# A second guessed expert, and 512-row units, in a fused attention and mixture-of-experts kernel

## The chip, the cores and the metric

The kernel runs on one core of a Trainium2 chip. The metric is device time in microseconds from launch to end; lower is better. Before and after are compared as medians of runs on the same chip. The engines are named as the profile names them: PE (TensorE, matmuls), ACT (ScalarE), DVE (VectorE), POOL (GpSimd, which issues the indirect transfers) and SP (SyncE, which issues the plain ones).

## What is computed

Three stages follow each other on 2304 tokens of 512 values. The cut reference:

```python
x = attn(q, k, v)                    # 4 x 8 heads, 576 positions, causal window of 64
h = maximum(x @ w_in, 0)             # 512 -> 2048
x = h * h @ w_out                    # 2048 -> 512, dense, all tokens
logits = x @ w_gate + modality_bias[modality_id]       # 8 experts
e_idx = argmax(logits); gate = max(softmax(logits))
for e in range(8):                   # top-1 mixture of experts
    m = e_idx == e
    out[m] = gate[m] * (maximum(x[m] @ w1[e], 0) @ w2[e])   # 512 -> 1024 -> 512
```

All arithmetic is fp32. The kernel gets it from matmuls on a high and a low part of each operand: three passes (high x high, high x low, low x high) stand for one product. Each weight chunk of 128 x 512 is therefore split on the way in, high part by ACT, low part by DVE (`split_hi`, `split_lo`), and so is each tile of activations (`xh`, `xl` and `hh`, `hl`).

## The kernel before

Attention and the dense layer run first, in groups of 256 and then of 512 rows. As the accumulators of the dense layer become ready, each block of 128 tokens goes through a gate (`gate_steps`, 18 blocks): DVE works out the logits and the expert, two tiny matmuls count places, POOL writes the token's number into a table in DRAM (`tbl`) at a place that belongs to its expert, and the row itself with its gate weight to `xs`. When all 18 blocks have passed, `list_steps` (DVE) makes a list of what remains to be done for which expert.

The expert layer works in units: a unit is a number of rows of one expert. For each unit the kernel looks up row numbers (`ix` from `tbl`), gathers the rows from `xs` with indirect transfers of 128 rows (POOL, `gather`), transposes them on PE (`transp`, tiles `ps_x`, then `xh` by ACT and `xl` by DVE), runs the layer (`moe2_job`, `run`), scales the results into a tile `o` (even blocks by ACT, odd by DVE, two buffers in the last part of the kernel) and scatters them to `out` with indirect transfers on POOL. `run` walks over groups `mp`: L1 matmuls of a group (`emit_L1`), its evacuation (`evac_L1`), then the L2 matmuls of the group before (`emit_L2`). Its `work` and `pieces` callbacks, called twice a group with a step number `s`, place everything else between the groups; tables in `KN` say at which step. For a 256-row unit a group is two slices of 128 hidden values, four groups in all; for 384 or 512 rows it is one slice, eight groups.

So that PE has work before the list is ready, three units of 256 rows (0, 1, 2) are guessed: they take the expert of the very first token, and rows of the first 14 blocks alone (`GUESS_TT`). Their indices and rows are fetched during the last dense group. What follows the guess is static: unit 2, unit 3 from the list, one wide unit `"w"` of 384 rows, units 4 to 7 from the list. If the list is longer, `extra` runs further units behind a branch. Each unit outside the guess loads its expert's 16 weight chunks (4 MB) while the unit before it runs; `ring` holds two experts.

The order on each engine comes from a scheduler in the language and from this program's order; all engines but PE's weight loads work through their queues in that order.

Of the kernel before, what the change touches and what calls it, by code (L numbers as in the profile page):

```python
# [1 line left out]
KN = {'at1': ((0, 3, 4, 5), (3, 6, 7, 8), (6, 9, 10, 11), (9, 12, 13, 14)),  # L2
# [4 lines left out]

# [47 lines left out]
def kernel(  # L55
# [14 lines left out]
    nc = tc.nc  # L70
# [474 lines left out]
    def gate_steps(tt, x2, per):  # L545
# [49 lines left out]
            nc.vector.tensor_copy(b0i, e0f)  # L595
        if tt == GUESS_TT - 1:
            t8 = small.tile([128, E], FP32, tag="t8", name="t8", bufs=1)
            nc.vector.tensor_tensor(out=t8, in0=noff, in1=base8, op=ALU.subtract)
            nc.vector.tensor_tensor(out=st0, in0=t8, in1=e0oh, op=ALU.mult)
            nc.vector.tensor_scalar(out=st0, in0=st0, scalar1=256.0 * GUESS, scalar2=None, op0=ALU.min)  # L600
# [148 lines left out]
    rows = {}  # L749
    late = {}  # L750

    def gather(u, base, n):
        assert state["n"] >= (GUESS_TT if u in range(GUESS) else NTT)
# [18 lines left out]
    turn = [len(GROUPS)]  # L772

    def transp(u):
        new_xT(("u", u), turn[0] % 2)
        turn[0] += 1
        xh, xl = xt_t["u", u]
        for hf in range(len(rows[u])):
            ps = bank([128, 4, 128], "ps_x")
            for kk in range(4):  # L780
                transpose(ps[:, kk, :], rows[u][hf][0][:, 128 * kk:128 * (kk + 1)])
            sl = (slice(None), slice(None), slice(128 * hf, 128 * hf + 128))
# [3 lines left out]
    def moe2_job(u):  # L786
# [6 lines left out]
        r = rows.pop(u)  # L793
# [179 lines left out]
    def last_work(s):  # L973
        if s == 0:
            dma_chunks(KN["nb"])
        if s >= KN['lsp']:
            split_steps(1)
        slot(2 if s < KN['lsp'] else 1)
        for u, at in enumerate(KN['lg']):
            if s == at:  # L980
                gather(u, bv0 + 256 * u, 128 * GUESS_TT)

    def last_pieces(s):
        if s == KN['lt']:
# [42 lines left out]
    def u_work(i, wide):  # L1027
        nxt = seq[i + 1] if i + 1 < len(seq) else None

        def f(s):  # L1030
            if nxt is None or (wide and s % 2):
                return
            s = s // 2 if wide else s
            if s == KN['g']:
                gather(nxt, evs[nxt], NT)
            split_steps(KN['sp' if i else 'sp0'][s])
            if s == KN['prep'] and i + 2 < len(seq):
                prep(seq[i + 2])
# [12 lines left out]
    tot = nc.values_load(toti[0:1, 0:1], min_val=0, max_val=LIST)  # L1051
# [66 lines left out]
```

## Time and profile before

| | |
|---|---|
| median of 3 runs | 736.81 us (733.63 to 736.97) |
| the profiled run's own time | 735.87 us |
| its span, first to last instruction | 734.2 us |
| mean granted clock of PE | 0.985 |
| PE busy | 699.3 us |
| DVE busy | 448.4 us |
| ACT busy | 356.8 us |
| POOL busy | 89.7 us |

The rows of the next section but one come from one execution. A line such as L477 is a line of the code above; a name left of the arrow is what an instruction writes, the names right of it what it reads. "Idle before" is how long the engine stood, with what it waited for.

### The profile page before, as it was taken

The page shows a single profiled execution, that of the slowest core. Times are in us where ns is not written, and L with a number is a line of the kernel's source. Part 1 is how long each engine was busy: PE and PEld are TensorE (multiplying, and loading weights), DVE is VectorE, ACT ScalarE, POOL GpSimd, SP SyncE. Part 2 cuts the span into 40 slices and gives each one's busy share as a digit, 9 for nine tenths or more (in the row PEclk, how much of TensorE's full clock was granted, in tenths as well). Part 3 has the DMA queues.
Part 4 walks back from the last instruction along what each step waited for, and adds up shares of the span by engine and source line. Part 5 has one row for each costly group of instructions (what it writes and reads, how often), then busy time and mean ns, then how long its engine had stood idle before and what let it go on. Part 6 is the DMA issues. An engine that isn't in the chain of part 4 may idle for free. (4 is left out here: it accounts for less than half of the span.)

```text
span 734.2 us, 13351 instructions
## 1 busy us (share of the span) xinstructions
PE 699.3 (95%) x4777; PEld 599.7 (82%) x4777; DVE 448.4 (61%) x1394; ACT 356.8 (49%) x841; POOL 89.7 (12%) x126
## 2 busy tenths in 40 slices
PE   6499999999999999999999999999996999999995
PEld 5398789888888888778888888888895988999994
DVE  3988997598665534685633794219846664477511
ACT  4867777565255345535434465433115553555410
POOL 3000000010000000010001110221313311112211
PEclk9899999999999999999999999999998999999998
DMA  7876651435222013204300168130248864577400
GB/s 209 278 235 203 197 178 37 169 108 115 42 69 80 30 50 66 66 30 79 80 31 5 68 60 127 30 87 16 53 60 264 270 201 160 173 239 248 144 29 21
DMA packets 62412, 84.49 MB, mean 115 GB/s; under 512 B 26016, under 2 KB 35248, under 8 KB 62208
## 3 DMA queue, kind: packets, MB, share of 16 engines
q1 hardware_dynamic: 57136, 69.26, 35.2%
q0 software_dynamic: 5200, 14.29, 6.1%
q8 instruction: 39, 0.64, 0.4%
q14 instruction: 37, 0.30, 0.1%
HBM read 74.23 MB, written 9.82 MB: 114 GB/s over the span
## 5 line engine op out<-in xcount | busy, mean ns | idle before, releaser
L477 PE MATMUL l<-xh,w 128*128 128x256 f32 (+2 forms) x1344 | 320.3, 320 | 0.0
L536 PE MATMUL acc<-w,hh 128*128 128x512 f32 x880 | 277.2, 395 | 0.0
L477 PEld LDWEIGHTS l<-xh,w 128*128 128x128 f32 x1344 | 228.5, 191 | 19.4 <-issue 1.5
L477 PE MATMUL l<-xl,w 128*128 128x256 f32 (+2 forms) x672 | 213.8, 318 | 0.0
L536 PEld LDWEIGHTS acc<-w,hh 128*128 128x128 f32 x880 | 160.0, 188 | 30.8 <-ACT hh L495 0.4
L536 PE MATMUL acc<-w,hl 128*128 128x512 f32 x440 | 172.3, 392 | 2.4 <-DVE hl L503 2.2
L477 PEld LDWEIGHTS l<-xl,w 128*128 128x128 f32 x672 | 128.4, 191 | 9.4 <-DVE xl L784 0.4
L489 ACT ACTIVATE hr<-l 128x512 f32<-128x512 f32 x72 | 42.7, 593 | 127.8 <-PE l L477 110.8
L503 DVE TENSOR_TENSOR hl<-hr,hh 128x512 fp32r<-128x512 f32 x72 | 49.7, 690 | 90.1 <-ACT hr L500 89.7
L536 PEld LDWEIGHTS acc<-w,hl 128*128 128x128 f32 x440 | 82.6, 188 | 22.1 <-DVE hl L503 3.1
L556 DVE CUSTOM_DVE_ANT_0 junk<-x,wgb 128x512 bf16<-128x512 f32 x144 | 98.9, 687 | 2.4 <-ACT x L742 0.2
L432 DVE TENSOR_TENSOR w<-st,w 128x512 fp32r<-128x512 f32 x112 | 72.1, 685 | 16.6 <-ACT w L429 16.4
L429 ACT CAST w<-st 128x512 fp32r<-128x512 f32 x112 | 63.8, 618 | 15.4 <-DMA st<-in_moe_w_dram 15.0
L274 ACT ACTIVATE p<-p,nm 128x128 f32<-128x128 f32 x144 | 55.9, 390 | 22.5 <-DVE nm L265 22.4
L516 ACT ACTIVATE hh<-l 128x512 fp32r<-128x512 f32 (+1 forms) x40 | 23.0, 574 | 82.5 <-PE l L477 82.5
L517 DVE SCALAR_TENSOR_TENSOR hl<-l,hh 128x512 fp32r<-128x512 f32 (+1 forms) x40 | 26.5, 662 | 58.8 <-ACT hh L516 58.5
L588 POOL DMA_DIRECT2D xs<-x x18 | 10.3, 574 | 304.4 <-DVE lg L556 145.9
L495 ACT ACTIVATE hh<-hr 128x512 fp32r<-128x512 f32 x72 | 45.5, 632 | 3.5 <-PE acc L536 1.5
L500 ACT ACTIVATE hr<-hr 128x512 f32<-128x512 f32 x72 | 45.5, 632 | 1.9
L585 POOL DMA_INDIRECT tbl<-tid,pi x18 | 19.4, 1079 | 159.4 <-DVE pi L582 123.1
L307 PE MATMUL ps_t<-ident,p 128*128 128x128 f32 x144 | 23.7, 291 | 12.9 <-DVE p L299 6.4
L307 PEld LDWEIGHTS ps_t<-ident,p 128*128 128x128 f32 x144 | 18.0, 149 | 17.0 <-ACT p L274 12.7
(146 smaller groups left out, 570.3 us busy)
## 6 DMA issues: line engine op xcount, KB each, us to landing
st<-in_moe_w_dram SPq DMA_DIRECT2D x112, 256.0 KB, 4.0
vt<-in_v_dram SPq DMA_DIRECT2D x35, 256.0 KB, 3.9
st<-in_moe_w_out_dram SPq DMA_DIRECT2D x16, 512.0 KB, 3.7
kt<-in_k_dram SPq DMA_DIRECT2D x17, 384.0 KB, 4.2
st<-in_moe_w_in_dram SPq DMA_DIRECT2D x12, 512.0 KB, 4.7
xs<-x POOLq DMA_DIRECT2D x18, 256.5 KB, 3.7
qt<-in_q_dram SPq DMA_DIRECT2D x36, 128.0 KB, 4.7
st<-in_moe_w_in_dram SPq DMA_DIRECT2D x8, 256.0 KB, 5.0
```

The costliest lines, as they stand in the source:

```text
L274: nc.scalar.activation(out=p[:, pr, :], in_=p[:, pr, :], func=ACTF.Exp, scale=-1.0, bias=nm[:, pr:pr + 1], accum_out=sm[:, pr:pr + 1])
L307: nc.tensor.transpose(out, in_, ident)
L429: nc.scalar.copy(out=part(where, 0, src), in_=src)
L432: eng.tensor_tensor(out=part(where, 1, src), in0=src, in1=part(where, 0, src).bitcast(FP32), op=ALU.subtract)
L477: nc.tensor.matmul(out=ps[:, job.cols * j:job.cols * (j + 1)], lhsT=wt[:, a, kk, f0:f0 + 128], rhs=job.x[b][:, kk, :], start=(kk == 0 and ...
L489: nc.scalar.activation(out=e["r"], in_=ps, func=ACTF.Relu)
L495: nc.scalar.activation(out=e["hh"], in_=e["r"], func=ACTF.Square)
L500: nc.scalar.activation(out=e["r"], in_=e["r"], func=ACTF.Square)
L503: nc.vector.tensor_tensor(out=hl, in0=e["r"], in1=e["hh"].bitcast(FP32), op=ALU.subtract)
L517: nc.vector.scalar_tensor_tensor(out=hl, in0=ps, scalar=0.0, in1=hh.bitcast(FP32), op0=ALU.max, op1=ALU.subtract)
L536: nc.tensor.matmul(out=job.acc[th], lhsT=h[a][:, c0:c0 + 128], rhs=wt[:, b, c, :], start=(mp == 0 and j == 0 and n == 0), stop=(mp == last ...
L556: nc.vector.tensor_tensor_reduce(out=gp["junk"], in0=x2[:, 0:DM], in1=gp["wgb"][:, e, :], scale=1.0, scalar=0.0, op0=ALU.mult, op1=ALU.add ...
```

## The change

A second expert is guessed. After block 13 the gate's counts say which expert other than the first token's has most rows; its number and table base go to `e1i` and `b1i`, and what is taken in advance from both experts goes to `st0`. Units 0, 1, 2 belong to the first, 3, 4, 5 to the second guessed expert. Units 0 and 1 run as one unit of 512 rows, and so do 3 and 4; the lookups of an expert's three units are one transfer of 768 indices (`guess_ix`). The sequence becomes (0, 1), 2, (3, 4), 5, `"w"`, 6, 7. The core of the diff:

```diff
-    U_MAX = GUESS + LIST
+    NGU = 2 * GUESS
+    U_MAX = NGU + LIST
...
         if tt == GUESS_TT - 1:
...
+            V.scalar_tensor_tensor(out=e1oh, in0=e0oh, scalar=-4096.0, in1=t8, op0=ALU.mult, op1=ALU.add)
+            V.scalar_tensor_tensor(out=e1oh, in0=e1oh, scalar=8.0, in1=rev8, op0=ALU.mult, op1=ALU.add)
+            V.tensor_reduce(out=e1f, in_=e1oh, axis=AX.X, op=ALU.max)
+            V.tensor_scalar(out=e1oh, in0=e1oh, scalar1=e1f, scalar2=None, op0=ALU.is_equal)
...
+            V.tensor_copy(e1i, e1f)
...
+            V.tensor_copy(b1i, e1f)
+            V.tensor_tensor(out=e1oh, in0=e0oh, in1=e1oh, op=ALU.add)
+            V.tensor_tensor(out=st0, in0=t8, in1=e1oh, op=ALU.mult)
...
+    def guess_ix(u, base):
+        t = late["row"].tile([128, 2 * GUESS], I32, tag="ixg", name="ixg", bufs=2)
+        nc.gpsimd.dma_start(out=t, in_=tbl[bass.ds(base, 256 * GUESS), :].rearrange("(h p) o -> p (h o)", p=128))
+        for k in range(GUESS):
+            ixs[u + k] = t[:, 2 * k:2 * k + 2]
...
-    def transp(u):
+    def transp(*us):
...
-        if u == "w":
-            job.n, job.fb, job.cols = 8, 1, WIDE
-        job.wkey = 0 if u in range(GUESS) else u
+        if u == "w" or len(us) == 2:
+            job.n, job.fb, job.cols = 8, 1, WIDE if u == "w" else 512
+        job.wkey = u // GUESS * GUESS if u in range(NGU) else u
...
-            if th == 0:
+            if th % 2 == 0:
                 nc.scalar.activation(out=o, in_=job.acc[th], func=ACTF.Copy, scale=t[:, DM:DM + 1])
...
+                if u == 0:
+                    guess_ix(0, bv0)
+                    bv1 = nc.gpsimd.value_load(b1i[0:1, 0:1], min_val=0, max_val=(E - 1) * EST)
+                    guess_ix(GUESS, bv1)
+                gather(u, None, 128 * GUESS_TT)
...
         if s == KN['lt']:
-            transp(0)
+            transp(0, 1)
...
-    run(moe2_job(0), u0_work, u_next(0))
-    run(moe2_job(1), u1_work, u_next(1))
+        if s == 8:
+            add_expert(GUESS, ev1)
+            dma_chunks(KN["nb"])
...
+    run(moe2_job(0, 1), u0_work, u0_pieces)
...
-    seq = list(range(GUESS - 1, U_STATIC))
-    seq.insert(KN["seqw"], "w")
-    prep(seq[1])
-    dma_chunks(KN["nb2"])
...
+    seq = [(2,), (3, 4), (5,), ("w",)] + [(u,) for u in range(NGU, U_STATIC)]
```

The steps at which gathers, weight splits and transposes are placed move too; two lines of the table:

```diff
+      'nb': 4, 'nb2': 6, 'rb': 6, 'ga': {(0, 1): ((3, 0), (4, 0)), (1, 1): ((5, 0),), (1, 8): (("w", 1),),
+      (2, 4): ((6, 1),), (3, 4): ((7, 1),)}, 'pr': {(1, 0): "w", (2, 2): 6, (3, 2): 7}, 'tt': (7, 13, 5, 10, 5),
```

What this does to the engines' order is seen at three places. In the rows below, line numbers of the kernel after are its own (L836 is the scatter that stands at L806 before, L793 the gather of L765, L791 the fill of L763, L834 the scaling of L804, L437 the low part of a weight chunk of L432, L522 the `hl` of L517). The first place is POOL around the start of unit 2. Before, the gather of unit 3 (`row_6081`, `row_6086`) stands ahead of unit 1's two scatters (`o_6063`, `o_6074`):

```order
L763 MEMSET row_6383 128x513
L763 MEMSET row_6388 128x513
L763 MEMSET row_6393 128x513
L765 DMA row_6081<-xs_87,ix_6079 128x513
L765 DMA row_6086<-xs_87,ix_6079 128x513
L806 DMA out_0_dram<-o_6063,ix_5259 2304x512
L763 MEMSET row_6690 128x513
L763 MEMSET row_6695 128x513
L806 DMA out_0_dram<-o_6074,ix_5259 2304x512
```

After, the first pair's four scatters (`o_5967` to `o_5991`) alternate with the fills and gathers of units 3 and 4 (`row_5996` to `row_6011`):

```order
L836 DMA out_0_dram<-o_5967,ixg_5225 2304x512
L791 MEMSET row_5996 128x513
L791 MEMSET row_6001 128x513
L793 DMA row_5996<-xs_87,ixg_5236 128x513
L793 DMA row_6001<-xs_87,ixg_5236 128x513
L836 DMA out_0_dram<-o_5975,ixg_5225 2304x512
L791 MEMSET row_6006 128x513
L793 DMA row_6006<-xs_87,ixg_5236 128x513
L836 DMA out_0_dram<-o_5983,ixg_5225 2304x512
L791 MEMSET row_6011 128x513
L793 DMA row_6011<-xs_87,ixg_5236 128x513
L836 DMA out_0_dram<-o_5991,ixg_5225 2304x512
```

Four scatters where two stood, and two of the gathers now stand behind scatters. The second place is DVE in the same stretch. Before, between the `hl` of unit 2's first group (`hl_6054`) and that of its second (`hl_6147`) stand one scaled block and three weight chunks:

```order
L517 SCALAR_TENSOR_TENSOR hl_6054<-l1_6028,hh_6053 128x512
L804 TENSOR_SCALAR o_6074<-acc_5817,row_5266 128x512
L432 TENSOR_TENSOR w_6091<-st_6016,w_6091 128x512
L432 TENSOR_TENSOR w_6091<-st_6018,w_6091 128x512
L432 TENSOR_TENSOR w_6091<-st_6020,w_6091 128x512
L517 SCALAR_TENSOR_TENSOR hl_6147<-l1_6095,hh_6146 128x512
```

After, the same two (`hl_5961`, `hl_6059`) have two scaled blocks between them (`o_5975`, `o_5991`: the second and fourth of the pair), the last directly ahead of `hl_6059`:

```order
L522 SCALAR_TENSOR_TENSOR hl_5961<-l1_5927,hh_5960 128x512
L834 TENSOR_SCALAR o_5975<-acc_5547,row_5243 128x512
L437 TENSOR_TENSOR w_5952<-st_5715,w_5952 128x512
L437 TENSOR_TENSOR w_5952<-st_5717,w_5952 128x512
L437 TENSOR_TENSOR w_6050<-st_5954,w_6050 128x512
L437 TENSOR_TENSOR w_6050<-st_5958,w_6050 128x512
L834 TENSOR_SCALAR o_5991<-acc_5549,row_5288 128x512
L522 SCALAR_TENSOR_TENSOR hl_6059<-l1_6024,hh_6058 128x512
```

The fourth block of the pair, which shares its `o` buffer with the second, has come to stand ahead of `hl_6059`. The third place is PE where unit 3's rows are transposed. Before, the eight transposes stand within unit 2, ahead of its last L1 group (`l_6251`):

```order
L536 MATMUL acc<-w,hh 128x512 x2
L536 MATMUL acc<-w,hl 128x512
L536 MATMUL acc<-w,hh 128x512 x2
L536 MATMUL acc<-w,hl 128x512
L307 MATMUL ps_x<-ident,row 128x128 x8
L477 MATMUL l_6251<-xh,w 128x256
L477 MATMUL l_6251<-xl,w 128x256
```

After, the sixteen of units 3 and 4 stand at the end of unit 2, ahead of the pair's first L1 group (`l_6223`, 512 columns), with the rest of unit 2's L2 around it:

```order
L541 MATMUL acc<-w,hl 128x512
L312 MATMUL ps_x<-ident,row 128x128 x16
L541 MATMUL acc<-w,hh 128x512 x2
L541 MATMUL acc<-w,hl 128x512
L541 MATMUL acc<-w,hh 128x512
L482 MATMUL l_6223<-xh,w 128x512
L541 MATMUL acc<-w,hh 128x512
L541 MATMUL acc<-w,hl 128x512
L541 MATMUL acc<-w,hh 128x512 x2
L482 MATMUL l_6223<-xl,w 128x512
```

The transposes have moved behind the unit's last L1 group, and L1 of the next unit follows them after four matmuls.

## Rows read from the trace of the kernel before

**Rows 1.** The profile's page: busy us, share of the span, instructions.

```profile
PE 699.3 (95%) x4777; PEld 599.7 (82%) x4777; DVE 448.4 (61%) x1394; ACT 356.8 (49%) x841; POOL 89.7 (12%) x126
```

**Rows 2.** Waits of PE's matmuls over the span: total us, times, longest.

```profile
PE ps_x L307 <- DMA row<-xs,ix: 6.2, 3, 5.4
...
PE ps_x L307 <- DMA row<-xs,ixw: 1.1, 1, 1.1
```

**Rows 3.** Four windows: us, busy PE PEld DVE ACT POOL, clock, DMA share, GB/s.

```profile
468.11:470.83 2.72, 2.72 (x14) 2.25 (x13) 0.73 (x2) 0.00 (x0) 0.00 (x0) 1.00 0.00 0
470.83:473.55 2.72, 2.72 (x14) 2.25 (x13) 0.57 (x1) 1.86 (x3) 0.94 (x2) 1.00 0.00 0
570.59:573.47 2.88, 2.88 (x26) 2.87 (x25) 2.37 (x4) 1.30 (x3) 0.00 (x0) 1.00 0.82 261
573.47:576.21 2.74, 2.74 (x14) 2.26 (x13) 0.69 (x1) 1.76 (x4) 0.20 (x1) 1.00 0.89 274
```

**Rows 4.** Timeline of PE, 556 to 568: start, us, instruction, idle before it.

```profile
556.04 0.39 PE L536 MATMUL acc<-w,hl 128*128 128x512 f32 x1
561.84 1.08 PE L307 MATMUL ps_x<-ident,row 128*128 128x128 f32 x4 [5.42 <-DMA row<-xs,ix]
563.45 1.11 PE L307 MATMUL ps_x<-ident,row 128*128 128x128 f32 x4 [0.53 <-DMA row<-xs,ix]
564.22 0.56 PE L477 MATMUL l<-xh,w 128*128 128x256 f32 x1
...
567.83 0.63 PE L536 MATMUL acc<-w,hh 128*128 128x512 f32 x2
```

**Rows 5.** Two windows behind that wait; the clock is third from the end.

```profile
561.84:564.22 2.38, 1.85 (x8) 1.45 (x9) 0.64 (x1) 0.58 (x1) 0.00 (x0) 0.50 1.03 401
564.22:567.83 3.61, 3.61 (x27) 3.61 (x25) 2.55 (x5) 2.15 (x4) 1.00 (x1) 0.80 0.40 129
```

**Rows 6.** Timeline of PE where eight transposes run unhindered.

```profile
489.87 1.03 PE L307 MATMUL ps_x<-ident,row 128*128 128x128 f32 x8
490.66 0.71 PE L536 MATMUL acc<-w,hh 128*128 128x512 f32 x2
```

**Rows 7.** Timeline of ACT behind the same transposes.

```profile
490.51 1.07 ACT L783 CAST xh<-ps_x 128x512 fp32r<-128x512 f32 x2 [1.24 <-PE ps_x L307]
```

**Rows 8.** Timeline of DVE behind the same transposes.

```profile
491.12 1.29 DVE L784 TENSOR_TENSOR xl<-ps_x,xh 128x512 fp32r<-128x512 f32 x2 [1.13 <-ACT xh L783]
```

**Rows 9.** Timeline of POOL: a first guessed gather, unit 3's gather, two scatters.

```profile
475.95 1.08 POOL L765 DMA_INDIRECT row<-xs,ix  x1 [1.11 <-DMA ix<-tbl]
...
554.82 1.12 POOL L765 DMA_INDIRECT row<-xs,ix  x1 [11.91 <-DMA ix<-tbl]
...
557.78 1.49 POOL L806 DMA_INDIRECT out_dram<-o,ix  x1 [0.30 <-issue]
...
565.19 1.00 POOL L806 DMA_INDIRECT out_dram<-o,ix  x1 [4.92 <-DMA out_dram<-o,ix]
```

**Rows 10.** Timeline of DVE at the end of the 384-row unit.

```profile
643.58 0.75 DVE L804 TENSOR_SCALAR o<-acc,row 128x512 f32<-128x512 f32 x1 [4.69 <-DMA out_dram<-o,ixw]
```

**Rows 11.** DMA issues from 541, 557.5, 637.5 and 724 on: us to landing.

```profile
st<-in_moe_w_dram SPq DMA_DIRECT2D x6, 256.0 KB, 8.7
...
out_dram<-o,ix POOLq DMA_INDIRECT x1, 7.1
...
out_dram<-o,ixw POOLq DMA_INDIRECT x1, 5.8
...
out_dram<-o,ix POOLq DMA_INDIRECT x1, 2.7
```

**Rows 12.** Groups by form: the two conversion steps of a weight chunk.

```profile
L432 DVE TENSOR_TENSOR w<-st,w 128x512 fp32r<-128x512 f32 x112 | 72.1, 685 | 16.6 <-ACT w L429 16.4
L429 ACT CAST w<-st 128x512 fp32r<-128x512 f32 x112 | 63.8, 618 | 15.4 <-DMA st<-in_moe_w_dram 15.0
```

**Rows 13.** Timeline of DVE: one small step at the end of block 13's gate.

```profile
464.31 0.17 DVE L599 TENSOR_TENSOR st<-t,e0oh 128x8 f32<-128x8 f32 x1
```

More of the change, by code (lines that the diff above doesn't have):

```diff
@@ L597, in gate_steps @@
             t8 = small.tile([128, E], FP32, tag="t8", name="t8", bufs=1)
[L598 to L600 removed]
+            e1oh = small.tile([128, E], FP32, tag="e1oh", name="e1oh", bufs=1)
+            e1f = small.tile([128, 1], FP32, tag="e1f", name="e1f", bufs=1)
+            V = nc.vector
+            V.tensor_tensor(out=t8, in0=noff, in1=base8, op=ALU.subtract)
+            V.scalar_tensor_tensor(out=e1oh, in0=e0oh, scalar=-4096.0, in1=t8, op0=ALU.mult, op1=ALU.add)
+            V.scalar_tensor_tensor(out=e1oh, in0=e1oh, scalar=8.0, in1=rev8, op0=ALU.mult, op1=ALU.add)
+            V.tensor_reduce(out=e1f, in_=e1oh, axis=AX.X, op=ALU.max)
+            V.tensor_scalar(out=e1oh, in0=e1oh, scalar1=e1f, scalar2=None, op0=ALU.is_equal)
+            V.tensor_tensor_reduce(out=nl, in0=e1oh, in1=iota8, scale=1.0, scalar=0.0,
+                                   op0=ALU.mult, op1=ALU.add, accum_out=e1f)
+            V.tensor_copy(e1i, e1f)
+            V.tensor_scalar(out=e1f, in0=e1f, scalar1=float(EST), scalar2=None, op0=ALU.mult)
+            V.tensor_copy(b1i, e1f)
+            V.tensor_tensor(out=e1oh, in0=e0oh, in1=e1oh, op=ALU.add)
+            V.tensor_tensor(out=st0, in0=t8, in1=e1oh, op=ALU.mult)
+            V.tensor_scalar(out=st0, in0=st0, scalar1=256.0 * GUESS, scalar2=None, op0=ALU.min)
         yield
@@ L750 @@
     late = {}
+    ixs = {}
+    def guess_ix(u, base):
[3 more added lines that the diff above has]
+            ixs[u + k] = t[:, 2 * k:2 * k + 2]
     def gather(u, base, n):
-        assert state["n"] >= (GUESS_TT if u in range(GUESS) else NTT)
+        assert state["n"] >= (GUESS_TT if u in range(NGU) else NTT)
         nh = 3 if u == "w" else 2
@@ L756, in gather @@
         pool = gp["wide"] if u == "w" else late["row"]
-        ix = late["row"].tile([128, nh], I32, tag="ix" + sfx, name="ix" + sfx, bufs=1 if u == "w" else 3)
-        eng = nc.gpsimd if u in range(GUESS) else nc.sync
-        eng.dma_start(out=ix, in_=tbl[bass.ds(base, 128 * nh), :].rearrange("(h p) o -> p (h o)", p=128))
+        if u in ixs:
+            ix = ixs.pop(u)
+        else:
+            ix = late["row"].tile([128, nh], I32, tag="ix" + sfx, name="ix" + sfx, bufs=1 if u == "w" else 3)
+            nc.sync.dma_start(out=ix, in_=tbl[bass.ds(base, 128 * nh), :].rearrange("(h p) o -> p (h o)", p=128))
         r = []
@@ L777, in transp, with moe2_job @@
         xh, xl = xt_t["u", u]
-        for hf in range(len(rows[u])):
+        for n, row in enumerate(r for v in us for r in rows[v]):
             ps = bank([128, 4, 128], "ps_x")
             for kk in range(4):
-                transpose(ps[:, kk, :], rows[u][hf][0][:, 128 * kk:128 * (kk + 1)])
-            sl = (slice(None), slice(None), slice(128 * hf, 128 * hf + 128))
+                transpose(ps[:, kk, :], row[0][:, 128 * kk:128 * (kk + 1)])
+            sl = (slice(None), slice(None), slice(128 * n, 128 * n + 128))
             nc.scalar.copy(out=xh[sl], in_=ps)
             nc.vector.tensor_tensor(out=xl[sl], in0=ps, in1=xh[sl].bitcast(FP32), op=ALU.subtract)
-    def moe2_job(u):
+    def moe2_job(*us):
+        u = us[0]
         job = Job()
         job.n, job.square = 4, False
-        if u == "w":
-            job.n, job.fb, job.cols = 8, 1, WIDE
-        job.wkey = 0 if u in range(GUESS) else u
+        if u == "w" or len(us) == 2:
+            job.n, job.fb, job.cols = 8, 1, WIDE if u == "w" else 512
+        job.wkey = u // GUESS * GUESS if u in range(NGU) else u
         job.x = [x[:, :, 0:job.cols] for x in xt_t.pop(("u", u))]
-        r = rows.pop(u)
+        r = [t for v in us for t in rows.pop(v)]
         def finish(th):
@@ L1020, in prep, with u_work, u_pieces @@
         add_expert(u, ev)
-    seq = list(range(GUESS - 1, U_STATIC))
-    seq.insert(KN["seqw"], "w")
-    prep(seq[1])
-    dma_chunks(KN["nb2"])
-    def u_work(i, wide):
-        nxt = seq[i + 1] if i + 1 < len(seq) else None
-        def f(s):
[L1031 to L1038, printed above, removed]
+    seq = [(2,), (3, 4), (5,), ("w",)] + [(u,) for u in range(NGU, U_STATIC)]
+    def u_work(i):
+        def f(s):
+            if seq[i] == ("w",):
+                if s % 2:
+                    return
+                s //= 2
+            for u, ev in KN['ga'].get((i, s), ()):
+                gather(u, evs[u] if ev else None, NT if ev else 128 * GUESS_TT)
+            split_steps(KN['spl'][i][s])
+            if (i, s) in KN['pr']:
+                prep(KN['pr'][i, s])
+                if not pend_split:
+                    dma_chunks(KN['nb2'])
         return f
-    def u_pieces(i, wide):
+    def u_pieces(i):
         def f(s):
-            if i + 1 < len(seq) and s == (KN['tw_'] if wide else KN['t0'] if i == 0 else KN['t']):
-                transp(seq[i + 1])
-        return f
-    for i, u in enumerate(seq):
-        run(moe2_job(u), u_work(i, u == "w"), u_pieces(i, u == "w"), u == seq[-1])
+            if i + 1 < len(seq) and s == KN['tt'][i]:
+                transp(*seq[i + 1])
+        return f
+    for i, us in enumerate(seq):
+        run(moe2_job(*us), u_work(i), u_pieces(i), us == seq[-1])
     settle(*PINNED)
@@ L1055, in extra @@
             return
-        with tc.If(tot > u - GUESS):
+        with tc.If(tot > u - NGU):
             prep(u)
```

18 lines of the change are left out of this document (9 added, 9 removed), and 3 rows, old and new, of the table KN.

## Prediction

> **What bounds the kernel now.** I read four views in this order. The page first: PE (TensorE) is busy for 95% of the span [rows 1], so a gain must come out of PE's idle time or of the number and size of its matmuls. Second PE's waits: after attention is done there is one kind of any size, the transposes of a unit's rows waiting for the gather of those rows, 6.2 us in three waits and 1.1 us in one [rows 2]. Third PE's timeline at the longest of them: matmuls run up to 556.04, the transposes of unit 3 start at 561.84 after 5.42 us idle, wait 0.53 us again for the second half, and L1 goes on at 564.22 [rows 4]. Unit 3 is the first that needs the list, so its chain is last table write, list, index lookup, gather; POOL itself sat 11.91 us waiting for the lookup before it could issue that gather at 554.82, which landed 7.0 us later [rows 9, 4]. Fourth the windows: the granted clock was 0.50 of full speed (1.2 GHz) while those transposes ran and 0.80 on average over the following group, after PE had done nothing for 5.42 us [rows 5]. Elsewhere from 490 on PE runs matmul behind matmul at clock 1.00, as in rows 3.
>
> **What the change removes.** (a) The long wait. From 556.27 (556.04 and the 0.23 us at which these matmuls follow each other, 2.72 us for 12 [rows 3]) to 564.22 are 7.95 us; eight transposes that wait for nothing take 0.79 us (489.87 to 490.66 [rows 6]). So 7.16 us go. The L1 group behind it took 3.61 us, to 567.83 [rows 4, 5], where the same group takes 2.88 [rows 3]: 0.73 more. The reason that both should go: units 3 to 5 now come from a guess, their indices are looked up before the first guessed unit starts, and the first unit that needs the list is the wide one, whose transposes now stand behind unit 2 and a 512-row unit, 66 us of matmuls after the list ends. (b) The short waits of the wide unit and of the one behind it, 1.1 and 0.25 us (6.2 less 5.42 and 0.53) [rows 2]: 1.3 us, since both are now looked up half a unit or more before their transposes.
>
> (c) Two pairs of units run as one. A 256-row unit is four groups of 24 L1 matmuls (2.88 us) and 12 L2 matmuls (2.74 us), 22.5 us, two of them 45.0. A 512-row unit is eight groups of 12 and 12, as the first stage has them: 8 x (2.72 + 2.72) = 43.5 [rows 3]. The gain is 1.44 a pair, or 1.1 if L2 takes the 2.74 us of a stretch with transfers and L1 stretches as much; I take 2.6 for both.
>
> The Trainium skill (TensorE: Matmul & The Clock Gate, "Back-to-back issue gap") gives N/2.4 + 2.5 ns for a full-speed matmul: 109 ns at 256 columns, 216 at 512, so a pair would save only 96 x 2.5 ns = 0.24 us. The trace says 120 and 227 ns here (2.88/24, 2.72/12) and decides.
>
> (d) Weight loads fall from seven experts to five: 32 fewer chunks, each 0.69 us of DVE and 0.62 us of ACT [rows 12]. Those engines are not what PE waits for, so nothing is booked; it is cover for what follows. (e) PE's work is otherwise the same: 19 transposed blocks, 2432 rows in all.
>
> **What it adds or moves.** (f) Ten more small DVE steps at the end of block 13's gate, 0.17 us each [rows 13], 2 us with their chaining. DVE has room there, and the POOL instruction that reads the result stands ahead of a lookup that waits for a table write anyway. Nothing. Behind it, POOL issues two lookups of 768 indices where it issued three of 256. The first gather stood at 475.95 [rows 9], the transposes at 489.87 [rows 6]; now the fourth gather must be in by then. Four gathers at 1.5 us (554.82 to 557.78 are two [rows 9]) and 7.0 us to land make 489 at worst. Nothing; a lookup 1 us later than before begins to cost one for one.
>
> (g) Sixteen transposes in a row before a 512-row unit, and L1 needs all four blocks. PE: 1.58 us, then four L2 matmuls, ready for L1 at 2.5 us. ACT begins 0.64 us after the transposes do, two copies take 1.07 us [rows 7], so the fourth ends at about 2.7; DVE starts 1.25 behind, 0.64 us each [rows 8], and is done at 3.8, when PE wants it at 3.7. So 0.3 us at each pair unit, between 0 and 1.0 if DVE still has gate work ahead of it.
>
> (h) The end of the first pair unit is where I expect a new wait. It has four row blocks, two `o` buffers and four scatters, and POOL issues a scatter only when the one before has landed: the scatter of 557.78 landed 7.1 us later, and the next went at 565.19 after 4.92 us idle [rows 9, 11]. DVE in turn waited 4.69 us for a scatter to land before it could write the third block of the wide unit [rows 10]. That cost nothing there, since no later `hl` was needed yet. Now DVE's fourth block stands ahead of the `hl` of unit 2's second group (order rows of DVE). Count from the start of the pair's last L2 group. PE needs that `hl` at 2.74 + 2.88 + 2.74 + 2.88 + 0.46 = 11.7. The first scatter goes at 0.69 + 0.75 = 1.4; the second when it has landed, and not before about 6 (its own 1.0 to 1.5 us, two gathers 2.96, two fills that I put at half a microsecond each); DVE's fourth block when the second has landed, then 0.75 and 0.69 for `hl`. With a landing of 2.7 us, as at the end of the kernel where nothing else moves [rows 11], it is ready at 10.1: no wait. With 5.8, as behind the wide unit, at 14.5: 2.8 us. With 7.1, as beside weight loads and gathers, at 17.1: 5.4 us. Unit 2 has twelve weight chunks and four gathers beside the scatters, which is nearest the middle row. I take 2.8, bounds 0 and 5.4. The four gathers of the second pair are issued between those scatters; by the same count the last goes at about 14.5, lands by 21.5, and is wanted at 23: no further wait.
>
> (i) In unit 2 the chunks of the second expert follow ACT and DVE, who are late by (h), and the first six go out while the last table write may still be in flight; the six at 541 took 8.7 us to land in such a place [rows 11]. ACT has two conversions ahead of the four copies of the transposed rows. If the last chunk is late by one step, the second pair starts late: 0 to 2.0 us, 0.9 taken between them, since I have no row nearer to one end.
>
> **Sum.** Gains 7.16 + 0.73 + 1.3 + 2.6 = 11.8. New waits 0.3 + 0.3 + 2.8 + 0.9 = 4.3. The profiled run took 735.87 us (span 734.2): 735.87 - 7.5 = 728.4. It lies 0.9 below the median of the three runs shown (736.81); I give 728.5.
>
> **Rivals.** *No new wait*: scatters land in about 3 us, only 0.6 of the new waits remain: 735.9 - 11.8 + 0.6 = 724.7. For it: DVE and ACT have 32 fewer conversions; against it: the landings of rows 11 beside transfers. The Trainium skill (DMA: Bandwidth & Descriptors, "Anatomy of one DMA — SWDGE (gpsimd) path") puts a transfer at 2.0 us plus bytes at 436 GB/s, 2.6 us for such a block; by that rule it would be this case. The trace agrees only where the queues are empty (2.7).
>
> *Long waits that eat most of the gain*, 7 to 12 us: landings of 7.1 in (h), 2.0 in (i), 1.0 at each pair, 9.4 in all: 733.5, in the band of no change (under 0.5%, 3.7 us, which is about what a measurement of this kernel can tell).
>
> *Slower, by the serial scatters*: with a landing L, `hl` is late by 2L - 8.8 once L is over 4.6. To eat 11.8 and 3.7 more, with the others of (g) and (i) at 4.0, the wait must be 11.5, so L at least 10.2 us in both scatters: 739.6 and up. The longest scatter among these rows is 7.1. Against it also that weight loads stop while DVE stands.
>
> *The guess doesn't hold*: if the second expert is not the one with most remaining rows, more than two listed units are left, and each runs behind the branch at the end with its load, conversion, gather and 22.5 us of matmuls uncovered: over 750. The reference's own inputs (first seed) give rows to two experts only, 1168 and 1136, of which 899 and 893 in the first 14 blocks; 768 of each are guessed, 400 and 368 remain, the wide unit takes the 368, and two units remain for the 400, exactly the static ones. No branch.
>
> **How the numbers follow.** Forecast case (new waits 2 to 7): 0.62. No new wait: 0.15. Long waits: 0.15, of which a little over half still under 733.1. Slower by scatters: 0.04. Guess: 0.04. Faster by over 0.5%: 0.62 + 0.15 + 0.09 = 0.86; same 0.06; slower 0.08. Range: 723.5 (no wait, and 1 us of spread) to 732.8 (all bounds of the forecast case).
>
> **What would show it.** The wait of 5.4 us before transposes is gone and the clock stays at 1.00 past 555. The two pair units show L1 groups of 2.72 us. In unit 2, DVE waits for `out_dram` and PE for `hl`, 0 to 5.4 us; between unit 2 and the second pair a wait for `xh` or the gather, under 3 us. I am wrong if PE waits longer than 5.4 us there, if the transposes of the first pair wait for rows, or if any unit runs behind the final branch.

## Result: faster by 1.1%, and the profile after

The changed kernel takes 727.07 us (median of 6 runs, 726.29 to 729.89), the kernel before in the same comparison 735.22 (6 runs, 732.77 to 737.90): ratio 0.9893, 95% interval 0.9862 to 0.9925. The profiled execution took 729.89 us, with a span of 728.2.

The page's first row: TensorE is as many per cent busy as before [rows 1], with 192 matmuls fewer.

```profile
PE 695.0 (95%) x4585; PEld 587.9 (81%) x4585; DVE 429.1 (59%) x1371; ACT 338.3 (46%) x810; POOL 88.3 (12%) x125
```

PE's waits (total us, times, longest). Behind attention only these two are left; the waits of transposes for gathered rows [rows 2] are gone.

```profile
PE acc L541 <- DVE hl L522: 1.0, 1, 1.0
PE acc L541 <- ACT hh L521: 0.9, 1, 0.9
```

PE's timeline there: the third group of unit 2, the first unit behind the first pair (L482 is L1, L541 L2, L312 the transposes).

```profile
552.88 0.28 PE L482 MATMUL l<-xh,w 128*128 128x256 f32 x1
554.08 0.73 PE L541 MATMUL acc<-w,hh 128*128 128x512 f32 x2 [0.93 <-ACT hh L521]
555.82 0.50 PE L541 MATMUL acc<-w,hl 128*128 128x512 f32 x1 [1.00 <-DVE hl L522]
...
558.22 0.28 PE L482 MATMUL l<-xh,w 128*128 128x256 f32 x1
```

Windows (columns as in [rows 3]): L1 and L2 of a 512-row unit, then the two groups with the waits, then two undisturbed groups of a 256-row unit.

```profile
571.59:574.40 2.81, 2.81 (x14) 2.26 (x13) 1.26 (x2) 0.46 (x1) 2.01 (x3) 1.00 0.19 80
574.40:577.13 2.73, 2.73 (x13) 2.25 (x12) 1.89 (x3) 1.62 (x3) 2.32 (x2) 1.00 0.32 87
550.12:554.08 3.96, 3.04 (x25) 2.82 (x23) 2.07 (x4) 3.31 (x7) 2.87 (x3) 1.00 0.22 89
554.08:558.22 4.14, 3.13 (x13) 2.28 (x13) 4.14 (x8) 2.51 (x5) 3.21 (x4) 1.00 0.77 188
616.86:619.74 2.88, 2.88 (x26) 2.87 (x25) 0.00 (x0) 0.94 (x2) 1.43 (x4) 1.00 0.22 91
619.74:622.48 2.74, 2.74 (x14) 2.26 (x13) 1.89 (x3) 1.27 (x3) 1.26 (x2) 1.00 0.47 152
```

The two waiting groups take 8.10 us where 5.62 (2.88 + 2.74) are due: 2.48 lost, at a granted clock of 1.00. What was late is read from ACT and then DVE (L832 and L834 write a scaled block to `o`, L434 and L437 convert weights):

```profile
542.65 0.69 ACT L832 ACTIVATE o<-acc,row 128x512 f32<-128x512 f32 x1
550.77 0.69 ACT L832 ACTIVATE o<-acc,row 128x512 f32<-128x512 f32 x1 [7.44 <-DMA out_dram<-o,ixg]
551.36 2.17 ACT L434 CAST w<-st 128x512 fp32r<-128x512 f32 x4
553.43 0.59 ACT L521 ACTIVATE hh<-l 128x512 fp32r<-128x512 f32 x1
```

```profile
552.01 2.50 DVE L437 TENSOR_TENSOR w<-st,w 128x512 fp32r<-128x512 f32 x4 [7.91 <-ACT w L434]
554.42 0.74 DVE L834 TENSOR_SCALAR o<-acc,row 128x512 f32<-128x512 f32 x1
555.08 0.68 DVE L522 SCALAR_TENSOR_TENSOR hl<-l,hh 128x512 fp32r<-128x512 f32 x1
```

ACT stands 7.44 us with the pair's third block, because both `o` buffers still wait for their scatters; four casts and the `hh` that PE wants stand behind it. DVE gets its weights from those casts, so its fourth block and `hl` are late next; that block itself waits for no scatter, it runs straight behind four weight chunks. POOL's timeline (answers [rows 9]) has the scatters (L836) and the gathers of the first pair and unit 2 (L793) behind their two lookups (L774):

```profile
474.79 1.75 POOL L774 DMA_DIRECT2D ixg<-tbl  x2 [8.03 <-DVE hl L508]
480.17 1.07 POOL L793 DMA_INDIRECT row<-xs,ixg  x1 [3.63 <-DMA ixg<-tbl]
...
486.84 1.01 POOL L793 DMA_INDIRECT row<-xs,ixg  x1 [0.30 <-issue]
...
543.62 1.00 POOL L836 DMA_INDIRECT out_dram<-o,ixg  x1 [4.92 <-ACT o L832]
...
550.94 1.02 POOL L836 DMA_INDIRECT out_dram<-o,ixg  x1 [2.76 <-DMA out_dram<-o,ixg]
...
554.51 1.02 POOL L836 DMA_INDIRECT out_dram<-o,ixg  x1 [0.30 <-issue]
...
560.57 1.32 POOL L836 DMA_INDIRECT out_dram<-o,ixg  x1 [2.70 <-DMA out_dram<-o,ixg]
```

The first scatter lands 7.2 us after its issue (550.77 less 543.62), the third some 6. The second, issued at 550.94, is no longer waited for when POOL reaches the third at 554.51, so it took 3.6 us at most. The windows of the first and the second (columns as above; the DMA share is the last but one) show what ran beside them: the DMA engines were busy for 84% of the first and 20% of the second.

```profile
543.62:550.77 7.15, 7.15 (x47) 6.50 (x46) 0.47 (x1) 0.00 (x0) 4.09 (x5) 1.00 0.84 311
550.94:554.51 3.57, 2.64 (x21) 2.31 (x19) 2.50 (x5) 3.57 (x8) 2.99 (x3) 1.00 0.20 81
```

**Where the time went.** Two stretches can be read in each profile (one profile of each kernel): from the first transposes of the expert stage to the last matmul (PE's timeline), and from the end of the last scatter's instruction (POOL's timeline) to the end of the span. The rows for the second, of the kernel before and of the changed one:

```profile
727.96 0.98 POOL L806 DMA_INDIRECT out_dram<-o,ix  x1 [2.51 <-DMA out_dram<-o,ix]
```

```profile
719.53 0.99 POOL L836 DMA_INDIRECT out_dram<-o,ix  x1 [2.47 <-DVE o L834]
```

In the table, "transposes" and "last matmul" are start times, "expert stage" is their difference and "tail" the second stretch, all in us:

```
                 transposes  last matmul  expert stage  tail   ratio to before (95%)
before             489.87      725.80        235.93      5.3
changed            490.69      717.41        226.72      7.7   0.9893 (0.9862-0.9925)
e1_o3              487.40      711.45        224.05      7.3   0.9857 (0.9831-0.9883)
e2_unpaired        488.50      713.37        224.87      7.9   0.9888 (0.9860-0.9915)
e3_merge_only      489.15      730.22        241.07      5.2   1.0056 (1.0034-1.0077)
e4_xswap           489.57      714.68        225.11      7.8   0.9898 (0.9875-0.9922)
e5_pad1            490.50      718.11        227.61      7.6   0.9879 (0.9837-0.9922)
e6_pad0            494.39      720.82        226.43      7.8   one run
e7_list13          493.71      721.68        227.97      5.8   0.9865 (0.9829-0.9900)
e8_small_first     490.31      716.05        225.74      7.8   one run
e9_three           493.03      717.07        224.04      5.9   0.9805 (0.9779-0.9831)
```

The expert stage is 9.2 us shorter, the tail 2.4 longer, and the stretch before the stage 0.8 longer in this execution (it varies by more between executions): 9.2 - 2.4 - 0.8 = 6.0, which is 735.87 less 729.89. The tail was in no term of the prediction. The stages of e5 and e7 hold a fall of the granted clock that those of the other kernels with the longer guess don't have; it is shown under e7.

### The profile page after: what moved, and what is told of

It reads as the page before. It is cut to its first block, busy times and chain, and to the rows that moved or that the text cites. A ratio compares the mean times of both kernels' runs of the same rounds, so it can differ in the third digit from the quotient of the medians.

```text
span 728.2 us, 12715 instructions
## 1 busy us (share of the span) xinstructions
PE 695.0 (95%) x4585; PEld 587.9 (81%) x4585; DVE 429.1 (59%) x1371; ACT 338.3 (46%) x810; POOL 88.3 (12%) x125
## 2 busy tenths in 40 slices
DMA packets 56953, 76.07 MB, mean 104 GB/s; under 512 B 24656, under 2 KB 33888, under 8 KB 56752
## 5 line engine op out<-in xcount | busy, mean ns | idle before, releaser
L482 PE MATMUL l<-xh,w 128*128 128x256 f32 (+2 forms) x1216 | 313.3, 336 | 0.0
L541 PE MATMUL acc<-w,hh 128*128 128x512 f32 x880 | 276.2, 395 | 1.0 <-ACT hh L521 0.9
L482 PEld LDWEIGHTS l<-xh,w 128*128 128x128 f32 x1216 | 211.4, 191 | 25.0 <-issue 1.7
L482 PE MATMUL l<-xl,w 128*128 128x256 f32 (+2 forms) x608 | 202.8, 334 | 0.0
L541 PEld LDWEIGHTS acc<-w,hh 128*128 128x128 f32 x880 | 160.9, 188 | 32.9 <-ACT hh L521 1.6
L541 PE MATMUL acc<-w,hl 128*128 128x512 f32 x440 | 172.5, 393 | 2.1 <-DVE hl L508 1.0
L482 PEld LDWEIGHTS l<-xl,w 128*128 128x128 f32 x608 | 116.2, 191 | 11.8 <-DVE xl L813 0.4
L541 PEld LDWEIGHTS acc<-w,hl 128*128 128x128 f32 x440 | 82.5, 188 | 22.0 <-DVE hl L508 2.7
L522 DVE SCALAR_TENSOR_TENSOR hl<-l,hh 128x512 fp32r<-128x512 f32 (+1 forms) x40 | 26.5, 662 | 78.5 <-ACT hh L521 76.0
L437 DVE TENSOR_TENSOR w<-st,w 128x512 fp32r<-128x512 f32 x80 | 51.9, 689 | 20.4 <-ACT w L434 20.1
L434 ACT CAST w<-st 128x512 fp32r<-128x512 f32 x80 | 45.7, 617 | 6.3 <-DMA st<-in_moe_w_dram 6.3
L593 POOL DMA_DIRECT2D xs<-x x18 | 10.3, 572 | 301.5 <-DVE lg L561 144.1
L312 PE MATMUL ps_t<-ident,p 128*128 128x128 f32 x144 | 23.5, 290 | 12.4 <-DVE p L304 5.3
L312 PEld LDWEIGHTS ps_t<-ident,p 128*128 128x128 f32 x144 | 17.9, 148 | 16.5 <-ACT p L279 12.2
```

The source lines that it names most:

```text
L312: nc.tensor.transpose(out, in_, ident)
L434: nc.scalar.copy(out=part(where, 0, src), in_=src)
L437: eng.tensor_tensor(out=part(where, 1, src), in0=src, in1=part(where, 0, src).bitcast(FP32), op=ALU.subtract)
L482: nc.tensor.matmul(out=ps[:, job.cols * j:job.cols * (j + 1)], lhsT=wt[:, a, kk, f0:f0 + 128], rhs=job.x[b][:, kk, :], start=(kk == 0 and ...
L522: nc.vector.scalar_tensor_tensor(out=hl, in0=ps, scalar=0.0, in1=hh.bitcast(FP32), op0=ALU.max, op1=ALU.subtract)
L541: nc.tensor.matmul(out=job.acc[th], lhsT=h[a][:, c0:c0 + 128], rhs=wt[:, b, c, :], start=(mp == 0 and j == 0 and n == 0), stop=(mp == last ...
```

## Experiments

The experiments ran on several chips, and the kernel before took 735.5 us on one and 738.6 to 739.0 on others. So times are compared by their ratio to the kernel before on the same chip, and stages by trace.

**e1_o3: a third output buffer.**

```
-                o = gp["wide"].tile([128, DM], FP32, tag="o", name="o", bufs=2)
+                o = gp["wide"].tile([128, DM], FP32, tag="o", name="o", bufs=3)
```

> One edit to the changed kernel: three output buffers `o` instead of two. Theory: the 2.48 us that PE loses in unit 2 (0.93 for `hh`, 1.00 for `hl`, the rest in the groups around them) come from ACT, which stands 7.44 us for an `o` buffer with the third row block of the first pair, and so holds the weight casts and the `hh` behind it. With a third buffer ACT goes on at once; DVE's fourth block then waits for the first scatter alone (until about 551), which is before the `hl` that PE wants. The waits for `hh` and `hl` go, and the time is 2.0 to 2.5 us below that of the changed kernel: about 724.8, ratio to the kernel before 0.985 to 0.987. Rival: the weight chunks of the second expert land too late, or the scatters are late for someone else; then ACT stands as long for a chunk as it did for the buffer, and the ratio stays at 0.989.

Measured 724.27 us, ratio 0.9857; the expert stage is 2.67 us shorter than that of the changed kernel, and PE waits for neither `hh` nor `hl`. ACT, and DVE's fourth block:

```profile
540.77 0.69 ACT L832 ACTIVATE o<-acc,row 128x512 f32<-128x512 f32 x1 [0.68 <-PE acc L541]
541.36 2.17 ACT L434 CAST w<-st 128x512 fp32r<-128x512 f32 x4
544.33 0.60 ACT L521 ACTIVATE hh<-l 128x512 fp32r<-128x512 f32 x1 [0.80 <-PE l L482]
```

```profile
546.65 0.75 DVE L834 TENSOR_SCALAR o<-acc,row 128x512 f32<-128x512 f32 x1 [3.35 <-DMA out_dram<-o,ixg]
```

The scatters are still slow (DVE waits until 546.65 for the one of 540.37, 6.3 us), but what stands behind that wait is done before PE needs it: the `hl` behind the block starts at 548.51, and the L2 group that reads it at 549.75. So the changed kernel's new wait was one for a buffer.

**e2_unpaired: the longer guess without the pairs.**

```
-            transp(0, 1)
+            transp(0)
...
-    run(moe2_job(0, 1), u0_work, u0_pieces)
+    run(moe2_job(0), u0_work, u_next(0))
+    run(moe2_job(1), lambda s: u0_work(s + 8), u_next(1))
...
-    seq = [(2,), (3, 4), (5,), ("w",)] + [(u,) for u in range(NGU, U_STATIC)]
+    seq = [(2,), (3,), (4,), (5,), ("w",)] + [(u,) for u in range(NGU, U_STATIC)]
```

The tables of steps move with it, to the single units' places.

> The changed kernel with the second expert guessed, but every unit of 256 rows on its own (no 512-row units). It tells what the pairs are worth, and leaves the longer guess alone. Theory from the trace: a pair gains 0.65 us (its L1 groups of 512 columns take 2.81, not 2.72), 1.3 for both; the pairs also cost 2.48 in unit 2 and 0.35 at the transposes of sixteen blocks. Without them the time is 1.3 - 2.8 = 1.5 us below the changed kernel: about 725.6, ratio 0.987, and PE waits for no `hh` or `hl` in unit 2. By the terms of the prediction (2.6 gained; 0.3 at each pair and 2.8 in unit 2 lost) it would be 0.8 below. Rival: the pairs are part of the gain (2.6 or more) and the wait in unit 2 is that of the scatters, which stay: then 2.6 slower than the changed kernel, 729.7, ratio 0.9925.

Measured 726.56 us, ratio 0.9888: by the time alone no different from the changed kernel. The stage, from one profile, tells more: 224.87, 1.85 us shorter than with pairs, and no wait in unit 2. So in this stage the guess alone is worth 235.93 - 224.87 = 11.1 us (its tail of 7.9 gives 2.6 back), and the pairs as they stand cost more than they give. In e1, where the pairs wait for nothing either, they give 224.87 - 224.05 = 0.82 for both.

**e3_merge_only: the first pair alone, on the kernel before.**

```
-            transp(0)
+            transp(0, 1)
...
-    run(moe2_job(0), u0_work, u_next(0))
-    run(moe2_job(1), u1_work, u_next(1))
+    run(moe2_job(0, 1), u0_work, u0_pieces)
```

> The kernel before with one thing of the change: units 0 and 1 run as one unit of 512 rows; one expert is guessed, as before, and unit 3 still needs the list. Theory: this alone does not gain, it loses. The four scatters of the pair now stand ahead of the lookup and the gather of unit 3 on POOL, each behind the landing of the one before, so that gather is issued at about 560 to 562 instead of 554.8, and PE's wait of 5.4 us grows to about 11: some 740, ratio 1.007. Rival A: the list alone sets that wait, the 0.65 or 1.3 us that the pair gains and what unit 2 loses both vanish in it: ratio 1.000. Rival B: a pair is worth 1.3 us wherever it stands: 733.9, ratio 0.998.

Measured 739.87 us, ratio 1.0056 (1.0034 to 1.0077): slower, by 5.1 us in the stage. POOL and then PE (L808 scatters, L765 gathers unit 3):

```profile
553.30 0.97 POOL L808 DMA_INDIRECT out_dram<-o,ix  x1 [1.47 <-DMA out_dram<-o,ix]
...
556.07 1.21 POOL L765 DMA_INDIRECT row<-xs,ix  x1 [1.25 <-DMA ix<-tbl]
557.92 1.41 POOL L808 DMA_INDIRECT out_dram<-o,ix  x1 [0.64 <-DMA out_dram<-o,ix]
559.63 1.05 POOL L765 DMA_INDIRECT row<-xs,ix  x1 [0.31 <-issue]
```

```profile
552.94 0.73 PE L536 MATMUL acc<-w,hh 128*128 128x512 f32 x2 [1.25 <-ACT hh L516]
554.60 0.50 PE L536 MATMUL acc<-w,hl 128*128 128x512 f32 x1 [0.92 <-DVE hl L517]
...
563.24 1.11 PE L307 MATMUL ps_x<-ident,row 128*128 128x128 f32 x4 [6.08 <-DMA row<-xs,ix]
565.79 1.12 PE L307 MATMUL ps_x<-ident,row 128*128 128x128 f32 x4 [1.43 <-DMA row<-xs,ix]
```

The direction and the sum are those of the theory, the way only in part. The first gather waits for its lookup, not for a scatter, and is 1.2 us late; the second stands behind the fourth scatter and is 3.4 us late; the theory had 6. The long wait grew from 5.42 and 0.53 to 6.08 and 1.43. The rest are the waits for `hh` and `hl`, another 0.9 us at the transposes of the two units that follow, and an L1 group behind the wait that ran at a lower clock for longer (4.80 us, where [rows 5] has 3.61):

```profile
566.56:571.36 4.80, 4.80 (x27) 4.80 (x26) 2.49 (x4) 2.14 (x4) 0.00 (x0) 0.56 0.25 87
```

**e4, e5, e6 and e8: why L1 takes 2.81 in the pairs.** The rows of a unit lie in turn in the buffers xT0 and xT1. Both pairs fall on xT1, and L1 groups of 512 columns in the first layer take 2.72 and 2.81 by the same buffer, in the kernel before too (its windows, xT1 and xT0):

```profile
312.11:314.92 2.81, 2.81 (x13) 2.21 (x12) 2.81 (x8) 0.99 (x2) 0.14 (x1) 1.00 0.26 96
478.99:481.71 2.72, 2.72 (x14) 2.25 (x13) 0.13 (x1) 0.00 (x0) 2.11 (x3) 1.00 0.70 178
```

```
e4  -    turn = [len(GROUPS)]
    +    turn = [len(GROUPS) + 1]
e5  +        xT_p[1].tile([128, 8], FP32, tag="pad", name="pad")
e6  +    xT_p[0].tile([128, 8], FP32, tag="pad", name="pad")
e8  +    small = ctx.enter_context(tc.tile_pool(name="small", bufs=2))
         ring = ctx.enter_context(tc.tile_pool(name="ring", bufs=8))
    ...
    -    small = ctx.enter_context(tc.tile_pool(name="small", bufs=2))
```

> The changed kernel with the two buffers of transposed rows in the other turn: the two pairs (and the wide unit) fall on the buffer xT0 where they had xT1, units 2, 5 and 7 the other way. Nothing else changes. Theory: L1 groups of 512 columns take 2.80 to 2.81 us whenever their rows lie in xT1 (also in the first layer's fourth block of rows, 302 to 404 us, in both kernels) and 2.72 in xT0, whatever DVE, ACT and the DMA queues do beside them. So the groups of both pairs fall to 2.72: 16 x 0.085 = 1.4 us less, 725.7, ratio 0.987. Rival: the expert weights, or the transfers and conversions beside them, make these groups slow; then they stay at 2.81 and the ratio at 0.989.

> The changed kernel with 32 unused bytes per partition ahead of the rows in the pool xT1, so that they start at 32 modulo 64 bytes, as those of xT0 do, and no longer at 0 (to make room one index buffer `ix` less: two instead of three). Theory: where the moving rows of 512 columns start within 64 bytes decides whether an L1 group takes 2.72 or 2.81 us. Then the groups of both pairs, and those of the first layer's fourth block of rows (302 to 404 us, also in xT1), fall to 2.72: 32 x 0.085 = 2.7 us less, 724.4, ratio 0.985. Rival: it is the place of xT1 in the memory as a whole, or something else that goes with that buffer; then the groups stay at 2.80 to 2.81 and the ratio at 0.989.

> The counterpart: the 32 unused bytes stand in the pool xT0, so that its rows start at 0 modulo 64 bytes, and those of xT1, which lie behind them, at 32 (again one `ix` buffer less). By the theory of the offset the two buffers change places: L1 groups of 512 columns take 2.81 in the first layer's third and last blocks of rows (xT0) and 2.72 in its fourth block and in the pairs (xT1); the time stays within 1 us, since 32 groups gain what 32 others lose. Rival: each buffer keeps its duration, 2.72 in xT0 and 2.81 in xT1.

> The changed kernel with the pool of small tiles (928 bytes) ahead of the ring of weights instead of behind the pool of `hh` and `hl`. The rows in xT1 stay where they were, the weights and the rows in xT0 move up by 928 bytes, so that the distance from a weight tile to the rows is a multiple of 2048 bytes in both buffers (in the changed kernel for xT0 alone; with 32 bytes ahead of xT0 that was broken, and its groups rose from 2.72 to 2.80). Theory: the distance between the moving rows and the weights, modulo the 2048 bytes of one row of 512 columns, decides; L1 groups of 512 columns then take 2.72 in xT1 too, in the pairs and from 302 to 404 us, and 32 x 0.085 = 2.7 us go from the time. Rival: the place of the buffer itself, or a larger stride than 2048, decides: 2.80 to 2.81 in xT1 as before.

One L1 group of a pair each, of e4 (in xT0), e5 (xT1) and e8 (xT1):

```profile
574.95:577.67 2.72, 2.72 (x13) 2.25 (x12) 0.00 (x1) 0.00 (x0) 1.31 (x2) 1.00 0.86 250
```

```profile
577.97:580.77 2.80, 2.80 (x13) 2.24 (x12) 0.00 (x0) 0.00 (x0) 1.30 (x2) 1.00 0.84 241
```

```profile
576.02:578.74 2.72, 2.72 (x13) 2.25 (x12) 0.00 (x1) 0.00 (x0) 1.31 (x2) 1.00 0.85 244
```

And e6: L1 of the first layer in xT0, and the L2 group ahead of it.

```profile
477.59:480.39 2.80, 2.80 (x14) 2.25 (x12) 0.05 (x1) 0.00 (x0) 1.69 (x2) 1.00 0.55 180
474.79:477.59 2.80, 2.80 (x13) 2.25 (x12) 0.64 (x1) 1.86 (x3) 0.07 (x1) 1.00 0.27 15
```

The buffer decides (e4), and the offset within 64 bytes does not (e5: still 2.80). In e6 the 32 bytes moved xT0, and `hh` and `hl` behind it, against the weights: L1 in xT0 rose to 2.80, and L2, where `hh` and `hl` are the stationary side, from 2.72 to 2.80. So neither of e6's two expectations came: the buffers did not change places, and xT0 did not keep its 2.72. In e8, where all distances to the weights are multiples of 2048 bytes, undisturbed L1 groups of 512 columns take 2.72, in xT1 from 302 to 404 us too, and so do the L2 groups of the pairs. By the addresses that the built programs give the tiles, L1 groups of 512 columns fit one rule in all eleven profiles: a distance of a multiple of 2048 bytes between weights and rows gives 2.72, the others tried (32, 864, 928 and 960 bytes off) 2.80 to 2.81. Which part of the memory or of PE makes it so is not shown.

The rule does not carry over to 256-row units. There the changed kernel's L1 groups take 2.88 in xT0, at a multiple of 2048 (616.86 above), and 2.85 in xT1, at 928 bytes off (unit 7):

```profile
692.60:695.45 2.85, 2.85 (x25) 2.85 (x24) 0.00 (x0) 0.00 (x0) 0.00 (x0) 1.00 0.00 0
```

In the time it is little: the ratio of e4, 0.9898 (0.9875 to 0.9922), shows none of the 1.4 us that were expected for the pairs (0.987). Its stage is 1.6 us shorter than that of the changed kernel.

**e7_list13: fewer nested branches.**

```
-    LIST = 16
+    LIST = 13
```

> The changed kernel with a list of 13 units instead of 16, so that 11 nested branches of extra units stand behind the static ones, as in the kernel before, and not 14 (none is taken for these inputs; longer lists are left out). From the end of the last scatter's instruction to the end of the span the kernel before takes 5.3 us, and the one with only a merged pair 5.2; the changed kernel and its three variants take 7.3 to 7.9. Theory: these 2.4 us are the way past the code of three more branches. Then the tail falls to 5.3 and the time to about 724.7, ratio 0.9857, with nothing else moved. Rival: the tail comes from something else of the change, such as the last scatters or the registers read at the end; then it stays above 7 us and the ratio at 0.989.

Measured ratio 0.9865. The last scatter and a span of 730.6 us leave a tail of 5.8:

```profile
723.80 0.99 POOL L836 DMA_INDIRECT out_dram<-o,ix  x1 [2.47 <-DVE o L834]
```

1.9 of the 2.4 us are gone. The intervals of the times overlap; the tail itself, 7.3 to 7.9 in seven profiles with 14 branches, 5.2 to 5.9 in the four with 11, settles that the length of the list decides. In that stretch the transfers of instructions (queue q14: count, MB, share) are three in each of the four profiles with 11 branches and four in each of the seven with 14. Before, changed and e7:

```profile
q14 instruction: 3, 0.02, 1.8%
q14 instruction: 4, 0.03, 1.5%
q14 instruction: 3, 0.02, 1.6%
```

That the one more transfer is what takes the 2 us is likely, but not shown.

The stage of e7 is 1.3 us longer than that of the changed kernel, though the edit leaves that stage alone. Its waits in unit 2 are alike (0.84 and 1.00 us), but behind them the granted clock fell, here and in e5 (0.62 and 1.00), to 0.70 over an L2 group of 5.71 us, where the changed kernel has 4.14 at 1.00:

```profile
557.04:562.75 5.71, 4.71 (x12) 3.43 (x13) 5.28 (x9) 3.73 (x7) 4.42 (x4) 0.70 0.81 242
```

**e9_three: third buffer, shorter list, small tiles first.**

> Three edits at once on the changed kernel: three `o` buffers, a list of 13 units, and the small tiles ahead of the weights. If each is worth what it showed alone (2.8 and 2.1 us) and the third is worth 2.7, the sum is 7.6 below the changed kernel: ratio to the kernel before 0.979. If the third is worth nothing: 0.9825. Rival: the gains don't add, since what ACT no longer waits for in unit 2 it waits for later; then 0.985 or more.

Measured 724.61 us against 738.95, ratio 0.9805 (0.9779 to 0.9831): better than both kernels. It lies in the middle between the full sum (0.979) and the sum without the third edit (0.9825), and its interval holds both, so what the third edit adds is not settled: the stage, 224.04, is no shorter than that of e1. PE still loses about 0.5 us in unit 2 there (0.24 in a wait for `hl`).

## Why the prediction came out right

The forecast of 728.5 (sum on its own execution: 7.5 gained) stands against 727.07. The trace gives 9.2 in the expert stage and -2.4 in the tail, 6.8 together. What was to go went, and a new wait came where it was expected; but that the total came so near is partly luck, since misses cancel. The guess gave 11.1 where 9.2 was booked, the pairs 1.3 instead of 2.6, the new waits cost 2.9 instead of 4.3, and 2.4 of the tail were booked nowhere: 7.1 in all, 0.3 more than the two stretches show.

- (a), (b) The waits for rows are gone, and the clock stays at 1.00 in this profile. Booked were 9.2 (7.9 and 1.3). Group by group, before against e2 gives 10.3: 6.06 in the L2 group that ended in the wait, 1.59 and 0.73 in the transposes and the L1 group behind it, 0.19 in the group ahead (8.6 for (a)); 1.32 and 0.44 at the two later units (1.8 for (b)). (a) left out that the two groups ahead of the wait already ran late, and (b) counted idle rows alone, without the transposes that ran slowly beside them. Another 0.7 come from slightly shorter L1 and L2 groups elsewhere.
- (c) This term failed. 2.6 was booked for two pairs from groups of 2.72; the pairs ran at 2.81 + 2.73, so 2 x 4 x (2.88 + 2.74) - 8 x 5.54 = 0.6 each, and e1 against e2 shows 0.8 for both, after the cost of (g). The 2.72 in [rows 3] was read in xT0, while the pairs fall on xT1; with the distance mended (e8) the predicted 2.72 + 2.72 is there. The 1.1 to 1.44 a pair were right for that layout. The 0.24 a pair that was estimated from the Trainium skill (TensorE: Matmul & The Clock Gate, "Back-to-back issue gap") fits neither layout.
- (d), (e) These hold: 76.07 MB were moved instead of 84.49, and PE waits for no weights.
- (f) This holds, at nothing: the first gather stood at 480.17, 4.2 us later than in [rows 9], all six were issued by 487.9, and the transposes at 490.69 waited for none. The forecast that a lookup over 1 us late costs one for one was too strict, by that margin.
- (g), (i) From the transposes to the next L1 group PE loses 0.27 us at the first pair (490.69 to 498.17, less 1.67 + 2.81 + 2.73) and 0.54 at the second; before single units at the same two places it loses 0.21 (kernel before) and 0.23 (e2). So these were 0.4 of new waits in place of 1.5.
- (h) Right in place, and right that scatters hold the two `o` buffers (e1 shows it); wrong in the path, and near in size (2.48 for 2.8) partly by luck. The step had two landings of equal length in a row, in front of DVE's fourth block. With the 7.2 of the first scatter in both it would have given 5.6. In fact PE's wait goes by one landing: ACT's third block stood for the buffer of the first scatter and held four casts and `hh` behind it, so `hh` was late before `hl`. The second landing took 3.6 at most, and DVE's block waited for neither. Over the six profiles with two `o` buffers and the pairs the loss in these two groups is 1.9 (e6) to 4.0 us (e7), inside the bounds of 0 and 5.4; the two largest, e5 and e7, hold the fall of the clock.
- Left out: the constant 3 guessed units became 6, the list kept its 16, so three more branches are nested behind the last unit: 2.4 us, of which e7 takes back 1.9.

Two of the signs that the prediction named did not come: the pair units' L1 groups of 2.72 us, and DVE waiting for a scatter in unit 2. And the range's upper end, 732.8, does not follow from the forecast case: its own limit of 7 us of new waits gives 731.1.

*No new wait* fell with the landing of 7.2 us. The Trainium skill (DMA: Bandwidth & Descriptors, "Anatomy of one DMA — SWDGE (gpsimd) path"), by whose figures it would be 2.6 (an estimate), does not hold beside weight loads here. *Slower by serial scatters* did not come, but e3 shows it in part: without the longer guess the same pair makes the kernel 0.56% slower, with one of the two gathers behind a scatter. The guess held: no unit ran behind a branch.

## What to carry to other kernels

A matmul's duration read in one stage holds for another only if its operands lie alike: compare windows buffer by buffer. When more blocks end at once than there are output buffers, ask which engine writes the first block without a buffer, and what stands behind it there. And look at what a changed constant does to code that never runs: here the way past it lay on the path to the end.

## What the hardware showed that was not expected

- The distance between weights and moving rows changes an L1 matmul of 512 columns by 3% (227 to 234 ns). The Trainium skill (SBUF — State Buffer, "SBUF: two separate sides") says that "PE, ACT, and DVE's dedicated pair never wait on anyone". That sentence is about engines that share ports, which no run here tests; it does not mention placement within the memory, which matters here.
- A list of 16 units instead of 13, with three more nested branches that are not taken, costs about 2 us at the end of the program. Whether each branch costs the same was not tried.
- Waits of 0.93 and 1.00 us left the granted clock at 1.00 in the changed kernel, but 0.84 and 1.00 in e7 and 0.62 and 1.00 in e5 were followed by 5.71 us at 0.70; one of 6.08 (e3) by an L1 group of 4.80 us at 0.56. What tells the first case from the next two is not shown.
